# Attention in pairs: the routing table's fill one store a chunk, scatters only behind it, early weights later

## The chip, the cores and the metric

The kernel runs on one core of a Trainium2 chip. The metric is the device time of one launch in microseconds (us); the time of a kernel is the median of several runs. Engines: TensorE (PE, matrix products; PEld is its weight load), VectorE (DVE), ScalarE (ACT), GpSimd (POOL) and SyncE (SP, which issues most DMAs).

## The reference

Three layers follow each other, all in float32. Batch 8, 8 heads, 576 positions, head width 64; afterwards 4608 tokens of width 512.

```python
# 1 retention: scores with a decay by distance, no softmax
ret = scale * (q @ k.T) * Dmat          # Dmat[i,j] = gamma_h**(i-j) for i >= j, else 0
x = (ret @ v)                           # then tokens x 512
# 2 top-1 mixture of 8 experts
logits = x @ w_gate + modality_bias[modality_id]
e_idx = argmax(logits); gate_w = softmax(logits)[e_idx]
out[mask] = gate_w[mask] * (relu(x[mask] @ w1[e]) @ w2[e])      # for each expert e
# 3 soft mixture of 8 experts with 4 slots each
logits = out @ phi
slot_input = softmax(logits, over tokens).T @ out
slot_out[e] = relu(slot_input[e] @ w1_[e]) @ w2_[e]
y = softmax(logits, over slots) @ slot_out
```

## The kernel before, in words

**Stages.** The attention stage computes x and the routing, the second stage the experts over at most 43 slots of 128 tokens, the third the soft mixture. The change lies in the attention stage alone.

**Chunks and pairs.** Two batch entries make 9 chunks of 128 tokens (8 of one entry each, and a ninth, shorter one of both ends), so there are 36 chunks `g`. The loop at `P_` handles two of them at a time: pair a has the chunks a and b = a+1, and the pairs are named here by their even chunk (pair 2, pair 4, ... pair 32; a last pair, 34, is written out behind the loop). In each pair stand, in this order: `loads(a); loads(b)`; `emit_v` for b and a+2 (line 167: vh, the scaled values, on GpSimd); score products `emit_S(a)` (line 176) and their masks (line 179, VectorE); products with the running state (`emit_cross`, line 200); gate logits of pair a−4; `emit_tok` of the pair before (line 218: x turned on TensorE, copied to xr by ScalarE at line 219, stored to xd in DRAM at lines 220 and 222); `emit_S(b)`; the gate products; values (`emit_AV`, line 205) and state products (`emit_state`, line 188, with ScalarE's state copy at line 189) in turn: AV(a), state(b), AV(b), state(a+2); the scaling of x (line 210); and pieces of the routing chain (`tick`, lines 232 to 259, among them r_ob at line 239 and the indices idx at line 257). Then come the scatters, and in pairs 24 to 30 `split`, which cuts a weight in `raw` into a high and a low part.

**Routing table.** `tb` in DRAM holds one row of 16 floats for each place of 128*324. `fill_tb` (line 156) writes the filler value into a ninth of it, from a tile `none` that shares its memory with `w2T1`. `scatter(k)` (lines 261 and 262) writes the 128 tokens of chunk k into their places by an indirect DMA of GpSimd, behind a small memset of `spare`. Rows of two scatters never meet, so scatters don't wait for each other; each waits for the fill and for its indices. A scatter's instruction stands in GpSimd's queue, in order, with the vh products. Four chunks are routed together: those of chunks 4k to 4k+3 can be scattered from pair 4k+8 on.

**DMA order.** SyncE issues its DMAs in the order of the program: `loads(g)` gives chunk g+5's kqv (7 buffers), then the extras that the change moves; the xd stores of the pair before come behind both. xr has 2 buffers, so a pair's xr copy waits until the store of the pair before has been read out. ScalarE is in order too: the state copies of a pair stand behind its two xr copies. state products accumulate in one PSUM tile, so state(a+2) waits for the state copy of b.

**Early weights.** `load_W(e)` brings expert e's w2T in four pieces of 0.5 MiB: e=0 into `w2`, e=1 into `w2T1`, e=2 into `raw` behind the splits, e=3 into kqv buffers. They are read behind the last pair. Four pieces of expert 0's w1 go into `raw` for the splits.

Of the kernel before, what the change touches and what calls it, by code (L numbers as in the profile page):

```python
# [80 lines left out]
def body(nc,tc,I,O):  # L81
# [3 lines left out]
    def nodep(ins,key):  # L85
        i=ins.ins if hasattr(ins,'ins') else ins
        if key in nodeps: tc.declare_no_dep(i,group=key,reason="the rows of one scatter differ from every other's")
        tc.add_to_no_dep_group(key,i); nodeps[key]=1
    ctx=ExitStack()
    with ctx, tc.manual_schedule():  # L90
# [8 lines left out]
        raw=[WP.tile([128,2048],F32,name=f"raw{j}") for j in range(2)]; w2=WP.tile([128,8,512],F32,name="w2")  # L99
# [18 lines left out]
        def load(g,xs=None):  # L118
            if g not in kqv: kqv[g]=A1.tile([128,4,512],F32,name="kqv",bufs=NKQ)
            for x,y in xs or ((0,3 if g%NCH==8 else 4),): SP.dma_start(out=kqv[g][:,x:y],in_=I['qkv'][g,:,x:y])  # L120
# [13 lines left out]
        def rest():  # L134
            SP.dma_start(out=cm[:,128:],in_=I['cm'][:,128:516]); SP.dma_start(out=tri,in_=I['tri']);
            SP.dma_start(out=mid,in_=I['mid'].bitcast(I32).rearrange("p (t w) -> p t w",w=2))
            SP.dma_start(out=mb.rearrange("p m e -> p (m e)"),in_=I['mb'].to_broadcast([128,2*E]))
        def decay(c):
            for h in range(2 if c==4 else 1):
                s=slice(64*h,64*h+64) if c==4 else slice(0,128); w=s.stop-s.start  # L140
                G_.tensor_tensor(out=gt[:,c,:,s],in0=gt[:,0,:,0:w],in1=bc(gr[:,:,c],[128,NP,w],2),op=ALU.mult)
# [14 lines left out]
        def fill_tb(): SP.dma_start(out=tb.rearrange("(k p c) w -> k p c w",p=128,k=TC//36)[tbk.pop(0)],in_=none)  # L156
# [5 lines left out]
        def tick(n=1,stop=True):  # L162
            for _ in range(n):
                if rq and not (stop and rq[0].__name__=="rank"): rq.pop(0)()
        def emit_v(g):
            t=A1.tile([128,H,D],F32,name="vh",bufs=3)
            G_.tensor_tensor(out=t,in0=kqv[g][:,2].rearrange("p (h d) -> p h d",h=H),in1=bc(vtab[:,pos_(g)],[128,H,D],2),op=ALU.mult)  # L167
            vh[g]=t
# [54 lines left out]
        def emit_logit(g):  # L223
            c=8*(g-max(k for k,_ in GR if k<=g))
            PE.matmul(out=psm[:,c:c+8],lhsT=lss[g//2][:,128*(g%2):128*(g%2)+128],rhs=sel[:,0:E],start=True,stop=True)
        rt={}
        def route_a(k0,n):
            ks=slice(k0,k0+n); sh=[128,n,E]
            def T(name,shape=sh,dt=F32): return A2.tile(shape,dt,name=name)
            l,mx,dl,ex,oh,ix,ob=T("r_l"),T("r_mx",[128,n]),T("r_d"),T("r_e"),T("r_oh"),T("r_ix",[128,n]),T("r_ob",dt=BF16)  # L230
            rt[k0]=(ex,ix,ob)
            return [lambda: V.tensor_tensor(out=l,in0=psm[:,0:n*E].rearrange("p (n e) -> p n e",e=E),in1=bias[:,ks],op=ALU.add),
                lambda: V.tensor_reduce(out=mx,in_=l,axis=AX.X,op=ALU.max),
                lambda: V.tensor_tensor(out=dl,in0=l,in1=bc(mx,sh,2),op=ALU.subtract),
                lambda: A.activation(out=ex,in_=dl,func=AF.Exp),

                lambda: V.scalar_tensor_tensor(out=oh,in0=dl,scalar=0.0,in1=bc(e8,sh,1),op0=ALU.is_equal,op1=ALU.mult),
                lambda: V.tensor_reduce(out=ix,in_=oh,axis=AX.X,op=ALU.max),
                lambda: V.tensor_tensor(out=ob,in0=bc(e8,sh,1),in1=bc(ix,sh,2),op=ALU.is_equal)]
        def route_b(k0,n):  # L240
            ks=slice(k0,k0+n); sh=[128,n,E]; ex,ix,ob=rt.pop(k0)
            def T(name,shape=sh,dt=F32): return A2.tile(shape,dt,name=name)
            rk=psm[:,40:40+n*E].rearrange("p (n e) -> p n e",e=E); rs,po,sm=T("r_rs"),T("r_po",[128,n]),T("r_sm",[128,n])
            r=[a for a,_ in GR].index(k0)
            if k0<GR[-1][0]: cn=T("r_cn",[128,E])
            def rank():
                PE.matmul(out=rk,lhsT=tri[:,:128],rhs=ob,start=True,stop=False)
                PE.matmul(out=rk,lhsT=tri[:,128:],rhs=bc(cum[:,r],sh,1),start=False,stop=n==1)
                for c in range(n-1): PE.matmul(out=rk[:,c+1:],lhsT=tri[:,128:],rhs=bc(ob[:,c],[128,n-1-c,E],1),start=False,stop=c==n-2)
            return [lambda: V.tensor_reduce(out=sm,in_=ex,axis=AX.X,op=ALU.add),  # L250
                lambda: V.tensor_scalar(out=sm,in0=sm,scalar1=1e-9,scalar2=None,op0=ALU.add),
                lambda: V.reciprocal(out=gk[:,ks,1],in_=sm),
                rank,
                lambda: V.tensor_tensor(out=rs,in0=rk,in1=ob,op=ALU.mult),
                lambda: V.tensor_reduce(out=po,in_=rs,axis=AX.X,op=ALU.add),

                lambda: V.scalar_tensor_tensor(out=idx[:,ks],in0=ix,scalar=float(36*128),in1=po,op0=ALU.mult,op1=ALU.add)]+([] if k0==GR[-1][0] else [
                lambda: V.tensor_reduce(out=cn,in_=ob.rearrange("p n e -> p e n"),axis=AX.X,op=ALU.add),  # L258
                lambda: V.tensor_tensor(out=cum[:,r+1],in0=cum[:,r],in1=cn,op=ALU.add)])
        def scatter(k):  # L260
            G_.memset(spare,0.0)
            nodep(G_.indirect_dma_start(out=tb,out_offset=bass.IndirectOffsetOnAxis(ap=idx[:,k:k+1],axis=0),in_=gk[:,k],in_offset=None),"tb")  # L262
# [6 lines left out]
        def load_W(e,cs=range(4)):  # L269
            if e not in w2T: w2T[e]={}  # L270
            for c in cs:
                if e in(3,5):
                    if c%2==0: w=A1.tile([128,2,1024],F32,name=f"w2T{e}",tag="kqv",bufs=NKQ); w2T[e].update({c:w[:,0],c+1:w[:,1]})
                elif e==2: w2T[e][c]=raw[c//2][:,c%2*1024:c%2*1024+1024]
                else: w2T[e][c]=(w2T1 if e==1 else w2)[:,2*c:2*c+2].rearrange("p a f -> p (a f)")
                SP.dma_start(out=w2T[e][c],in_=I['w2T'][e,:,c])
# [14 lines left out]
        scat=[]  # L291
        def logit(g):
            emit_logit(g)
            def f(k0,n): rq.extend(route_a(k0,n)+[lambda: rq.extend(route_b(k0,n)+[lambda: scat.extend(range(k0,k0+n))])])
            for k0,n in GR[:-1]:
                if g==k0+n-1: f(k0,n)
        def loads(g):
            if g==0: load(4)
            if g+5<NT: load(g+5)
            if 4<=g<10: fill_tb(); fill_tb() if g%2 else 0  # L300
            if g==1: rest()
            if g==5: SP.dma_start(out=phi,in_=I['phi'])
            if 10<=g<26 and g%2==0: load_W((g-10)//8,[(g-10)//2%4])
            if g in(15,17,19,21): x,y=divmod(g//2-7,2); SP.dma_start(out=raw[x][:,1024*y:1024*y+1024],in_=I['w1'][0,:,x,1024*y:1024*y+1024])
            if g in(30,31,33): load_W(2,{30:[0],31:[1],33:[2,3]}[g])
            if g in(32,33): load_W(3,range(2*g-64,2*g-62))
        emit_v(0); emit_S(0); emit_state(0)
        for P_ in range(NT//2-1):
            a,b=2*P_,2*P_+1; ready=rq and rq[0].__name__=="rank"
            loads(a); loads(b)  # L310
            emit_v(b); emit_v(a+2)
            for g in (a,b):
                if g<4: decay(g+1)
            for _ in range(3 if a==4 else 2):
                if prepare and a: prepare.pop(0)()
            if a: emit_S(a)
            emit_cross(a); emit_cross(b)
            for g in (a-4,b-4):
                if g>=0: logit(g)
            if ready: tick(1,False)  # L320
            if a: emit_tok(a-2); emit_tok(b-2)
            tick(4)
            emit_S(b)
            if a: emit_gate(P_-1)
            emit_AV(a)
            if b%NCH<8: emit_state(b)
            emit_AV(b)
            if (a+2)%NCH<8: emit_state(a+2)
            emit_x(a); emit_x(b)
            tick(14)  # L330
            for _ in range(2):
                if scat: scatter(scat.pop(0))
            for g in (a,b):
                if 24<=g<32: split((g-24)//4,[(g-24)%4])

# [8 lines left out]
        a,b=NT-2,NT-1; ready=rq and rq[0].__name__=="rank"  # L344
# [258 lines left out]
        for i in range(NSURE):  # L603
            slot(i)
            x,h=divmod(i-12,2)
# [114 lines left out]
```

## Time and profile before

| what | us |
|---|---|
| median of 3 runs (650.27 to 654.31) | 653.67 |
| the profiled execution, whole | 657.15 |
| its span, first to last instruction | 655.1 |
| TensorE busy in the span | 598.1 |
| of the span: from the start of pair 4 to that of pair 34 | 24.53 to 156.26 |

The profile is of one execution. Times in its rows count from the start of the span. Busy time of an engine leaves out its queue's waits; "idle before" is the time in which an engine stood, and the name behind the arrow is what ended it by the profile: of several things waited for, the one that came last among those that the trace shows. A DMA's landing has no row of its own; a SyncE row is the issue alone.

### The profile page before, as it was taken

What the parts mean: (1) busy time and instruction counts of PE and PEld (TensorE: products, weight loads), DVE (VectorE), ACT (ScalarE), POOL (GpSimd) and SP (SyncE); (2) the same over time, 40 slices, a digit from 0 to 9 for tenths busy, and PEclk for the clock granted to TensorE, in tenths of its full rate; (3) what the DMA queues carried; (4) which work ended last, traced back from release to release, by engine and by line L of the source; (5) the groups of instructions that cost most, each with busy time, mean ns of one, the idle gap of its engine ahead of it and who ended that gap; (6) DMA issues with size and microseconds to landing.
All of it is one profiled execution on the core that took longest, in us unless ns stands there. A gap on an engine that the chain in (4) does not pass through costs nothing. (4 is left out here: it accounts for less than half of the span.)

```text
span 655.1 us, 17160 instructions
## 1 busy us (share of the span) xinstructions
PE 598.1 (91%) x6005; PEld 445.0 (68%) x6005; DVE 317.2 (48%) x952; ACT 202.6 (31%) x528; POOL 239.3 (37%) x347
## 2 busy tenths in 40 slices
PE   7996999999796999998899999999999999769984
PEld 5775888887465667775577777777776777543553
DVE  1554666666523343566354555544556445422343
ACT  1212222332124233264223332332345223212232
POOL 3614555543444323366233433444346333210000
PEclk7999999999899899998899999999999999989995
DMA  8999999999358570036634444434335401399888
GB/s 306 405 409 403 362 395 416 410 347 336 101 181 313 193 307 17 21 99 217 245 133 160 163 166 165 148 129 152 140 101 165 154 20 28 108 354 388 334 288 289
DMA packets 48243, 148.47 MB, mean 227 GB/s; under 512 B 12276, under 2 KB 24063, under 8 KB 37888
## 3 DMA queue, kind: packets, MB, share of 16 engines
q1 hardware_dynamic: 41936, 132.54, 55.1%
q0 software_dynamic: 6192, 14.53, 6.2%
q8 instruction: 57, 0.93, 0.6%
q14 instruction: 58, 0.48, 0.2%
HBM read 276.14 MB, written 27.71 MB: 464 GB/s over the span
## 5 line engine op out<-in xcount | busy, mean ns | idle before, releaser
L489 PE MATMUL ps_L<-wh,xl 128*128 128x512 f32 x624 | 211.4, 409 | 0.1
L489 PEld LDWEIGHTS ps_L<-wh,xl 128*128 128x128 f32 x624 | 115.9, 191 | 36.8 <-issue 16.3
L489 PE MATMUL ps_L<-wl,xl 128*128 128x512 f32 x312 | 127.0, 407 | 12.2 <-POOLq L546 6.3
L489 PEld LDWEIGHTS ps_L<-wl,xl 128*128 128x128 f32 x312 | 59.3, 190 | 41.2 <-POOL cy L525 16.1
L493 DVE TENSOR_SCALAR hh<-ps_L,gi 128x512 f32<-128x512 f32 x39 | 29.3, 750 | 101.0 <-PE ps_L L489 101.0
L511 ACT ACTIVATE z<-ps_z,mt 32x128 f32<-32x128 f32 x39 | 14.0, 358 | 156.5 <-DVE mt L510 156.5
L179 DVE TENSOR_TENSOR st_s<-ps_s,cm 128x512 f32<-128x512 f32 x72 | 46.2, 683 | 31.2 <-PE ps_s L176 18.3
L525 POOL TENSOR_SCALAR cy<-cx,cm 128x32 f32<-128x32 f32 x39 | 15.0, 384 | 121.1 <-DVE cm L524 117.2
L262 POOL DMA_INDIRECT tb<-gk,idx x36 | 35.6, 988 | 53.8 <-DVE r_cn L258 30.6
L167 POOL TENSOR_TENSOR vh<-kqv,vtab 128x512 f32<-128x512 f32 x36 | 37.2, 1040 | 40.3 <-PE ps_x L205 25.3
L526 POOL DMA_INDIRECT cs<-cy,ui x39 | 43.0, 1103 | 16.9 <-POOL cy L525 13.3
L176 PE MATMUL ps_s<-kqv 64*128 64x128 f32 x576 | 45.8, 294 | 0.0
L498 PE MATMUL ps_h<-cs__100,hh 128*128 128x128 f32 x312 | 41.3, 275 | 1.2 <-DVE hh L493 1.2
L219 ACT COPY xr<-ps_t 128x512 f32<-128x512 f32 x36 | 20.2, 587 | 71.0 <-DMA xd<-xr 23.2
L176 PEld LDWEIGHTS ps_s<-kqv 64*128 64x128 f32 x576 | 38.0, 195 | 6.0 <-issue 2.7
L205 PE MATMUL ps_x<-st_s,vh 128*64 128x128 f32 x576 | 40.0, 281 | 0.0
L210 DVE TENSOR_TENSOR xT<-ps_x,gt 128x512 f32<-128x512 f32 x36 | 23.2, 686 | 33.7 <-PE ps_x L205 32.0
L205 PEld LDWEIGHTS ps_x<-st_s,vh 128*64 128x64 f32 x576 | 32.0, 139 | 7.5 <-issue 7.2
L498 PEld LDWEIGHTS ps_h<-cs__100,hh 128*128 128x128 f32 x312 | 35.6, 142 | 1.8 <-DVE hh L493 1.6
L470 POOL DMA_INDIRECT xr__2796<-xd,ui x28 | 29.3, 1047 | 16.4 <-POOL ui L469 7.8
L492 ACT ACTIVATE hh<-ps_L,gi 128x512 f32<-128x512 f32 x39 | 26.9, 689 | 25.9 <-PE ps_L L489 25.7
L469 POOL CAST ui<-gi 128x1 uint32<-128x1 f32 x42 | 7.6, 182 | 67.8 <-DMA cs<-cy,ui 56.9
(234 smaller groups left out, 967.6 us busy)
## 6 DMA issues: line engine op xcount, KB each, us to landing
raw<-in_w SPq DMA_DIRECT2D x79, 1024.0 KB
w<-in_w SPq DMA_DIRECT2D x38, 2048.0 KB
kqv<-in_qkv SPq DMA_DIRECT2D x28, 1024.0 KB
m<-in_m SPq DMA_DIRECT2D x19, 1024.0 KB
xd<-xr SPq DMA_DIRECT2D x32, 256.0 KB
w2T<-in_w2T SPq DMA_DIRECT2D x12, 512.0 KB
out<-m SPq DMA_DIRECT2D x12, 512.0 KB
mx<-in_m SPq DMA_DIRECT2D x5, 1024.0 KB
```

The source lines that it names most:

```text
L167: G_.tensor_tensor(out=t,in0=kqv[g][:,2].rearrange("p (h d) -> p h d",h=H),in1=bc(vtab[:,pos_(g)],[128,H,D],2),op=ALU.mult)
L176: r=slice(64*h,64*h+64); PE.matmul(out=pss[h][:,p],lhsT=pk(g,0)[r,p],rhs=pk(g,1)[r,p],start=True,stop=True)
L179: V.tensor_tensor(out=st,in0=pss[h],in1=bc(masks[g%NCH],[128,NP,128],1),op=ALU.mult)
L205: PE.matmul(out=xo(g,p,h),lhsT=v[:,2*p+h],rhs=sts[g,h][:,p],start=False,stop=p>1,skip_group_check=True)
L210: V.tensor_tensor(out=of(xTs[g//2],g).rearrange("q (h n) t -> q h n t",h=2),in0=xps[g//2][:,:,256*(g%2):256*(g%2)+256].rearrange("q h (n t ...
L262: nodep(G_.indirect_dma_start(out=tb,out_offset=bass.IndirectOffsetOnAxis(ap=idx[:,k:k+1],axis=0),in_=gk[:,k],in_offset=None),"tb")
L470: G_.indirect_dma_start(out=xg[i%3],out_offset=None,in_=xd,in_offset=bass.IndirectOffsetOnAxis(ap=u,axis=0),bounds_check=NTOK-1,oob_is_err ...
L489: PE.matmul(out=ps,lhsT=a[:,c],rhs=w[h][:,s],start=n==0,stop=n==11); n+=1; m+=1
L492: if h==0: A.activation(out=d,in_=q,func=AF.Relu,scale=g)
L493: else: V.tensor_scalar(out=d,in0=q,scalar1=0.0,scalar2=g,op0=ALU.max,op1=ALU.mult)
L498: for c in range(4): PE.transpose(out=ps[:,c],in_=hh[i%2][:,2*half+c//2,(c%2)*128:(c%2)*128+128],identity=ident)
L526: nodep(G_.indirect_dma_start(out=cs,out_offset=bass.IndirectOffsetOnAxis(ap=gi[i][1],axis=0),in_=y,in_offset=None,bounds_check=NTOK-1,oob ...
```

## The change

Three things, all in the pair loop. The nine fill stores, issued at chunks 4 to 9 (one at even, two at odd chunks), are issued at chunks 5 to 13, one each. The scatters, up to two a pair from pair 8 on, are up to three a pair from pair 14 on. Weight pieces move: experts 0 and 1 of w2T from the even chunks 10 to 24 to chunks 20, 21, 23, 24, 26, 27, 29 and 30; the four pieces of w1 from chunks 15, 17, 19, 21 to 14, 15, 17, 18; expert 2 of w2T from chunks 30, 31, 33 (1, 1 and 2 pieces) to 32 and 33 (2 each).

```diff
+        W1_=[14,15,17,18]; W01=[20,21,23,24,26,27,29,30]
         def loads(g):
             if g==0: load(4)
             if g+5<NT: load(g+5)
-            if 4<=g<10: fill_tb(); fill_tb() if g%2 else 0
+            if 5<=g<14: fill_tb()
             if g==1: rest()
             if g==5: SP.dma_start(out=phi,in_=I['phi'])
-            if 10<=g<26 and g%2==0: load_W((g-10)//8,[(g-10)//2%4])
-            if g in(15,17,19,21): x,y=divmod(g//2-7,2); SP.dma_start(out=raw[x][:,1024*y:1024*y+1024],in_=I['w1'][0,:,x,1024*y:1024*y+1024])
-            if g in(30,31,33): load_W(2,{30:[0],31:[1],33:[2,3]}[g])
+            if g in W01: k=W01.index(g); load_W(k//4,[k%4])
+            if g in W1_: x,y=divmod(W1_.index(g),2); SP.dma_start(out=raw[x][:,1024*y:1024*y+1024],in_=I['w1'][0,:,x,1024*y:1024*y+1024])
+            if g in(32,33): load_W(2,range(2*g-64,2*g-62))
             if g in(32,33): load_W(3,range(2*g-64,2*g-62))
...
             tick(14)
-            for _ in range(2):
-                if scat: scatter(scat.pop(0))
+            if a>13:
+                for _ in range(3):
+                    if scat: scatter(scat.pop(0))
```

On GpSimd, from pair 6 on, the queue before had the first scatters right behind pair 8's vh products (`DMA tb` is a scatter, 41472 the rows of the table):

```order
L167 TENSOR_TENSOR vh<-kqv,vtab 128x512 x4
L261 MEMSET spare 1x1
L262 DMA tb<-gk,idx 41472x16
L261 MEMSET spare 1x1
L262 DMA tb<-gk,idx 41472x16
L167 TENSOR_TENSOR vh<-kqv,vtab 128x512 x2
L261 MEMSET spare 1x1
L262 DMA tb<-gk,idx 41472x16
```

Now, at the same place:

```order
L167 TENSOR_TENSOR vh<-kqv,vtab 128x512 x10
L261 MEMSET spare 1x1
L262 DMA tb<-gk,idx 41472x16
L261 MEMSET spare 1x1
L262 DMA tb<-gk,idx 41472x16
L261 MEMSET spare 1x1
L262 DMA tb<-gk,idx 41472x16
L167 TENSOR_TENSOR vh<-kqv,vtab 128x512 x2
```

The vh products of pairs 10 to 14 now stand ahead of the first scatter, and three scatters stand between the vh products of pairs 14 and 16.

On SyncE, from pair 4's loads to pair 8's first one, the queue before was (`tb<-w2T_98` is a fill store):

```order
L120 DMA kqv<-in_qkv 128x2048
L156 DMA tb<-w2T_98 128x576
L120 DMA kqv<-in_qkv 128x2048
L156 DMA tb<-w2T_98 128x576 x2
L302 DMA phi<-in_phi 128x128
L220 DMA xd<-xr 128x512 x2
L120 DMA kqv<-in_qkv 128x2048
L156 DMA tb<-w2T_98 128x576
L120 DMA kqv<-in_qkv 128x2048
L156 DMA tb<-w2T_98 128x576 x2
L220 DMA xd<-xr 128x512 x2
L120 DMA kqv<-in_qkv 128x2048
```

Now:

```order
L120 DMA kqv<-in_qkv 128x2048 x2
L156 DMA tb<-w2T_98 128x576
L303 DMA phi<-in_phi 128x128
L220 DMA xd<-xr 128x512 x2
L120 DMA kqv<-in_qkv 128x2048
L156 DMA tb<-w2T_98 128x576
L120 DMA kqv<-in_qkv 128x2048
L156 DMA tb<-w2T_98 128x576
L220 DMA xd<-xr 128x512 x2
L120 DMA kqv<-in_qkv 128x2048
```

Ahead of the xd stores of pair 6 stand three fill stores instead of six.

## Rows read from the trace of the kernel before

**Rows 1.** The page's first line.
```profile
span 655.1 us, 17160 instructions
```

**Rows 2.** Stretches cut at pair starts: us, busy by engine, clock, DMA share, GB/s.
```profile
24.53:34.29 9.76, 7.89 (x136) 6.62 (x132) 4.88 (x8) 2.09 (x5) 6.76 (x11) 1.00 1.01 408
34.29:41.91 7.62, 7.62 (x135) 6.45 (x132) 3.34 (x8) 1.92 (x6) 1.04 (x1) 1.00 1.04 414
41.91:51.75 9.84, 8.09 (x155) 6.88 (x153) 6.41 (x18) 2.01 (x6) 1.07 (x2) 1.00 1.02 400
51.75:64.32 12.57, 8.95 (x151) 7.60 (x148) 4.08 (x10) 2.31 (x6) 5.54 (x9) 0.94 1.01 404
64.32:73.91 9.59, 9.59 (x140) 8.02 (x138) 6.88 (x15) 2.19 (x5) 6.20 (x9) 0.90 0.99 365
73.91:89.76 15.85, 15.85 (x304) 13.84 (x301) 9.61 (x27) 4.14 (x10) 7.90 (x12) 1.00 1.00 367
89.76:129.97 40.21, 39.61 (x707) 34.06 (x703) 25.53 (x66) 11.81 (x29) 21.32 (x32) 1.00 1.02 415
```

**Rows 3.** TensorE in order of time: start, us, instruction, idle before and releaser.
```profile
51.14 0.69 PE L188 MATMUL ps_st<-vh,kqv 128*64 128x64 f32 x16 [1.36 <-issue]
...
61.72 0.69 PE L188 MATMUL ps_st<-vh,kqv 128*64 128x64 f32 x16 [3.62 <-POOL vh L167]
...
64.32 2.08 PE L176 MATMUL ps_s<-kqv 64*128 64x128 f32 x16
...
73.91 1.16 PE L176 MATMUL ps_s<-kqv 64*128 64x128 f32 x16
```

**Rows 4.** GpSimd in order of time.
```profile
58.14 1.18 POOL L262 DMA_INDIRECT tb<-gk,idx  x1 [14.94 <-DVE st_s L179]
...
60.62 2.04 POOL L167 TENSOR_TENSOR vh<-kqv,vtab 128x512 f32<-128x512 f32 x2
...
65.17 2.04 POOL L167 TENSOR_TENSOR vh<-kqv,vtab 128x512 f32<-128x512 f32 x2
...
81.69 1.04 POOL L167 TENSOR_TENSOR vh<-kqv,vtab 128x512 f32<-128x512 f32 x1 [0.30 <-PE ps_x L205]
...
85.87 1.01 POOL L262 DMA_INDIRECT tb<-gk,idx  x1 [3.12 <-DVE r_cn L258]
...
88.91 2.04 POOL L167 TENSOR_TENSOR vh<-kqv,vtab 128x512 f32<-128x512 f32 x2 [0.75 <-PE ps_x L205]
```

**Rows 5.** ScalarE in order of time.
```profile
49.25 1.23 ACT L219 COPY xr<-ps_t 128x512 f32<-128x512 f32 x2 [7.06 <-DMA xd<-xr]
...
50.65 0.39 ACT L189 COPY st<-ps_st 128x256 f32<-128x256 f32 x1
...
77.94 1.07 ACT L219 COPY xr<-ps_t 128x512 f32<-128x512 f32 x2 [3.55 <-PE ps_t L218]
```

**Rows 6.** SyncE in order of time: issues of DMAs.
```profile
40.94 1.00 SPq L220 DMA_DIRECT2D xd<-xr  x2
...
47.03 1.35 SPq L156 DMA_DIRECT2D tb<-w2T  x2
```

**Rows 7.** VectorE in order of time.
```profile
45.68 0.16 DVE L257 SCALAR_TENSOR_TENSOR idx<-r_ix,r_po 128x4 uint32<-128x4 f32 x1
...
64.99 2.27 DVE L239 TENSOR_TENSOR r_ob<-cm,r_ix 128x32 bf16<-128x32 f32 x1
...
83.06 0.19 DVE L239 TENSOR_TENSOR r_ob<-cm,r_ix 128x32 bf16<-128x32 f32 x1
```

**Rows 8.** The page's DMA issues: how many, KB each.
```profile
kqv<-in_qkv SPq DMA_DIRECT2D x28, 1024.0 KB
...
xd<-xr SPq DMA_DIRECT2D x32, 256.0 KB
...
tb<-w2T SPq DMA_DIRECT2D x9, 288.0 KB
...
raw<-in_w SPq DMA_DIRECT2D x4, 512.0 KB
```

## The prediction

> **What bounds the kernel now.** I read the page first: the profiled execution spans 655.1 us and took 657.15 us; three timed runs have a median of 653.67 us [rows 1]. The change touches only the attention stage, so the next view is the table of stretches, cut at the starts of the pairs (a pair starts with the first score matmul of its even chunk) [rows 2]. A pair that nothing holds takes TensorE 7.62 us (the stretch from 34.29). Pair 8 takes 9.84, pair 10 takes 12.57 and pair 12 takes 9.59: 2.22, 4.95 and 1.97 too long. In all of them the DMA share is about 1.0 at 400 to 414 GB/s, so the queue is full as well; that matters below.
>
> Two chains make those losses. The order in time on TensorE shows the first state matmuls of pair 8's end starting at 51.14 after 1.36 us of idle, and those of pair 10 at 61.72 after 3.62 us waiting for vh [rows 3].
> - **Scatter behind the fill.** On GpSimd the first scatter starts at 58.14 after 14.94 us of idle; behind it in the same queue stand the vh products that pair 10 needs, which run at 60.62 [rows 4]. The row names VectorE as releaser, but the scatter's indices were written at 45.68 [rows 7]. What else it needs is the table it writes into: the last two fill stores were issued at 47.03 [rows 6]. So the wait is for the fill to land, some 10 us after issue.
> - **Row store ahead of the state copy.** ScalarE's copy xr at 49.25 waited 7.06 us for an xd store, and the state copy stands behind it at 50.65 [rows 5]; TensorE needs that one at 51.14. The xd store in question was issued at 40.94 [rows 6]: 8.3 us from issue until the buffer was free, which at the 400 to 408 GB/s of that stretch is about 3.3 MB ahead of it in the queue.
>
> Pair 12's loss is a consequence: after the 3.62 us of idle the granted clock of pairs 10 and 12 is 0.94 and 0.90 in the mean [rows 2], and 16 score matmuls take 2.08 us where they take 1.16 in pair 14 [rows 3], close to the ratio of the 1.2 and 2.4 GHz levels. VectorE's r_ob also took 2.27 us instead of 0.19 while two vh products ran [rows 4, 7].
>
> **The change part by part.**
>
> *The scatters leave pairs 8 to 12.* Six scatters of about 1.2 us each (two of them fill the time from 85.87 to 88.16, 0.75 us ahead of the vh at 88.91 [rows 4]) go to later pairs, and with them the wait of 14.94 us. vh of pair 10 then runs right behind that of pair 8. Of pair 10's 4.95 us I keep 0.3 for what is late next, the xr copy (below): 4.65 us saved. Without the idle the clock doesn't fall and r_ob meets no late vh: of pair 12's 1.97 us I keep 0.3 too: 1.67 us.
>
> *The fill spread thin.* A pair issues two kqv loads of 1 MiB and two xd stores of 0.25 MiB [rows 8]; the fills of 0.28 MiB come on top: three in each of pairs 4, 6 and 8 before, one, two, two, two, two in pairs 4 to 12 now. At pair 6's xd store 0.84 MiB (0.88 MB) less has been issued: at 408 GB/s it lands 2.2 us earlier, so pair 8's xr runs at 47.1 instead of 49.25. TensorE without its 1.36 us of idle would have been ready at 49.78, and copy to state takes 51.14 − 49.25 = 1.9 us, so xr is in time until 47.9, 6.0 us after the pair's start. The wait goes; I keep 0.2 of the pair's 2.22: 2.0 us. Pair 4's long 9.76 us stays: its xr waits for stores that stand ahead of the first fill in both kernels.
>
> Sum of the early part: 2.0 + 4.65 + 1.67 = 8.3 us.
>
> *The weights later.* The queue is what may take this back. A pair of 7.62 us at 408 GB/s moves 2.97 MiB; 2.5 are kqv and xd, so 0.47 MiB of extras fit. Extras in MiB, pairs 4 to 32: before 0.84, 0.84, 0.84, 0.5, 0.5, then 1, 1, 1, 1, 0.5, 0.5, 0, 0, 1, 3; now 0.28, 0.56, 0.56, 0.56, 0.56, then 1, 0.5, 0.5, 1, 0.5, 0.5, 1, 0.5, 0.5, 4. In pairs 14 to 24 the new kernel brings 4.0 MiB for a room of 2.8 + 0.25 (one short kqv chunk): 0.95 MiB over, 2.4 us. Before it was 5.0 MiB, 1.95 over, 5.0 us; but its queue had run partly dry during the stalls: 365 and 367 GB/s over 25.4 us [rows 2] are about 1.05 MB less than 408 would be, 2.6 us. So both come to the same 2.4 us. What differs is where they start: before, xr of pair 14 ran at 77.94, 4.0 us after the pair's start and unhurried [rows 5]; now it will stand about 5.5 us after it, near the limit. That 1.5 us of slack is used up, so later pairs pay up to 1.5 us more: between −1.5 (all of it paid) and 0 (the five pairs from 89.76 at 8.04 us a pair had waits of their own [rows 2], which then may shrink). I take −1.4, nearest to the ledger.
>
> The four weight pieces put into raw at chunks 14 to 18 come before the splits of pair 24 need them. Pieces 20 to 30 are read only behind the last pair. All 4 MiB at pair 32 (3 before) stand ahead of its xd stores, 2.6 us more; no state copy follows in the last pair, so 0 to −1, taken as 0.
>
> *Three scatters a pair from pair 14.* Three cost 3.6 us, two vh 2.04 [rows 4]: 5.6 of 7.62 us on GpSimd, so vh is not held up by number. What is queued behind the first scatter is pair 16's vh, and TensorE waits for that. The last fill is now issued in pair 12, which starts at about 41.9 + 7.8 + 7.9 = 57.6; with the old latency of 58.14 − 47.03 = 11 us it lands near 68.5, while GpSimd gets there soon after pair 14's start, at 66. Three scatters then end near 72, some 1 us after vh could have begun, and vh is not needed until about 5 us later. The one thing in its way is r_ob of pair 16: 83.06 in the old trace, when GpSimd was past its vh [rows 7]. Bounds 0 and 2.27 − 0.19 = 2.1 us; I take 0.3, since only part would overlap. A 27th scatter inside the loop takes one from the end, where they wait for the last indices anyway: 0.
>
> Result: 8.3 − 1.4 − 0.3 = 6.6 us. For the profiled execution 657.15 − 6.6 = 650.5; for the median 653.67 − 6.6 = **647.1 us**. Nothing behind the attention stage changes, so the gain should arrive whole.
>
> **Rivals.**
> - *Nothing is given back.* The waits of the later pairs (8.04 against 7.62 us [rows 2]) shrink as much as the lost slack costs: 8.3 us, at most 10 with some of those waits gone: 645.4. For it: 2 MiB less has been issued by pair 18. Against it: the DMA share stays at 1.0 there. Chance 0.16.
> - *The queue gives back more.* If 365 to 367 GB/s from 64 to 90 us is not a dry queue but what it gives with scatters and weights together, the new kernel meets that rate too and loses the 2.6 us of the ledger: gain 4.0, 649.7. Against it: 415 GB/s in the next five pairs, with scatters and weights [rows 2]. Chance 0.22. The Trainium skill's rule on this speaks against the change as a whole: in "DMA: Bandwidth & Descriptors", section Bandwidth, the share of one core binds loads from HBM near 358 GB/s. By that share a pair would move 2.6 MiB, the room for extras would be 0.1, and every pair of either kernel would stand at the queue. The 366 GB/s of these two stretches come near it; the 400 to 415 of the others disagree, and the same page gives 425 to a core that streams alone.
> - *GpSimd's late vh blocks VectorE.* In pair 12 r_ob stood for 2.27 us beside two vh products. In pair 16 the second vh ends at 81.69 + 1.04 = 82.73 and r_ob starts at 83.06: 0.3 us between [rows 4, 7]. If the third scatter puts vh later than that in the five pairs that route (16, 20, 24, 28, 32), each pays what pair 12 paid, 1.97 us: −9.9, so 6.6 − 9.9 = −3.3: 657.0, slower. It decides from vh starting over 0.3 us later than now; the 5.6 us of work in 7.62 speak against it. Chance 0.05. The skill states such a lock in "SBUF — State Buffer", section Who interferes with whom: VectorE with two SBUF inputs and a GpSimd operation that reads SBUF exclude each other; the row on r_ob agrees.
> - *The change doesn't do what it says.* If the first scatter waited for something other than the fill, the wait returns at pair 14 with its 4.65 and 1.67 us: gain 8.3 − 6.3 = 2.0 less the queue's 1.4: 653.1. Against it: no other operand was late. Chance 0.06.
>
> **How the numbers follow.** The forecast case, gain 5 to 8 us (645.7 to 648.7), has 0.51. About 1% (6.5 us) is what a measurement of this kernel tells from no change. Over that lie the first rival (0.16) and somewhat over half of the forecast (0.29): faster 0.45. Within lie the rest of the forecast (0.22), the second rival (0.22) and the last (0.06): same 0.50. Slower 0.05. The range runs from 643.5 (nothing given back and 1.7 of the later waits gone) to 651.5 (the second rival with 1 us at the end and 0.8 of collision).
>
> **What would show it.** Right: no idle of GpSimd ahead of a scatter before pair 14 and under 4 us there; TensorE's waits for vh from pair 10 on gone; pairs 8, 10, 12 between 7.6 and 8.0 us with clock 1.00; xr in pairs 12 to 24 still waiting for xd. Wrong: pairs 14 to 30 longer than before by over 3 us in sum, a DMA rate under 395 GB/s there, r_ob near 2 us in several pairs, or a new wait of TensorE at pair 16.

## The result and the profile after

Timed beside the kernel before, the changed kernel took 647.98 us in the median of 10 runs (646.22 to 648.78), the kernel before 653.99 us (10 runs, 650.27 to 656.13): a ratio of 0.9908, with a 95% interval of 0.9886 to 0.9931. The forecast was 647.1 us. Two later sets of runs, each on one chip with its own runs of the kernel before, did not repeat it: 660.02 against 657.25 us (1.0037, 1.0016 to 1.0058) and 658.91 against 657.48 us (1.0022, 1.0002 to 1.0042). So there are two things to explain: why the forecast came out, and why the gain went away elsewhere.

The profiled execution of the first measurement took 648.3 us; its page begins:

```profile
span 646.5 us, 17164 instructions
```

The stretches that answer to [rows 2], cut at the starts of pairs 4, 6, 8, 10, 12, 14, 18 and 28, with the same columns:

```profile
25.80:35.59 9.79, 7.90 (x137) 6.62 (x133) 4.88 (x8) 2.10 (x5) 6.76 (x11) 1.00 1.01 410
35.59:43.20 7.61, 7.61 (x135) 6.45 (x132) 3.34 (x8) 2.31 (x6) 1.04 (x1) 1.00 1.04 376
43.20:51.47 8.27, 7.88 (x156) 6.88 (x154) 5.39 (x16) 1.82 (x4) 2.33 (x3) 1.00 1.02 410
51.47:59.55 8.08, 8.08 (x152) 7.02 (x148) 4.70 (x12) 2.31 (x6) 2.08 (x3) 1.00 1.03 414
59.55:67.33 7.78, 7.78 (x142) 6.72 (x138) 5.05 (x16) 2.19 (x5) 2.09 (x3) 1.00 1.02 388
67.33:84.49 17.16, 16.87 (x306) 14.14 (x302) 10.66 (x27) 4.12 (x10) 10.45 (x17) 1.00 1.02 404
84.49:125.36 40.87, 39.75 (x707) 33.97 (x703) 25.49 (x66) 11.77 (x29) 25.20 (x39) 1.00 1.02 396
```

Pairs 8, 10 and 12 fell from 9.84, 12.57 and 9.59 us to 8.27, 8.08 and 7.78, with the clock at 1.00; pairs 14 and 16 grew from 15.85 to 17.16, and the five behind them from 40.21 to 40.87.

On TensorE, in order of time (as [rows 3]), the state products at the ends of pairs 8 and 10 no longer stand idle first:

```profile
50.91 0.64 PE L188 MATMUL ps_st<-vh,kqv 128*64 128x64 f32 x16
...
58.99 0.63 PE L188 MATMUL ps_st<-vh,kqv 128*64 128x64 f32 x16
```

GpSimd in order of time (as [rows 4]), the first scatters and the vh behind them:

```profile
71.98 1.18 POOL L262 DMA_INDIRECT tb<-gk,idx  x1 [3.84 <-DMA kqv<-in_qkv]
...
73.46 0.97 POOL L262 DMA_INDIRECT tb<-gk,idx  x1 [0.20 <-issue]
...
74.74 0.96 POOL L262 DMA_INDIRECT tb<-gk,idx  x1 [0.22 <-issue]
75.72 2.06 POOL L167 TENSOR_TENSOR vh<-kqv,vtab 128x512 f32<-128x512 f32 x2
```

SyncE's last fill store (as [rows 6]), and r_ob of pair 16 on VectorE (as [rows 7]):

```profile
62.55 0.34 SPq L156 DMA_DIRECT2D tb<-w2T  x1
```

```profile
76.77 1.06 DVE L239 TENSOR_TENSOR r_ob<-cm,r_ix 128x32 bf16<-128x32 f32 x1
```

The first scatter waits 3.84 us, until 9.4 us behind the last fill's issue, and vh follows the three scatters while r_ob runs beside it. ScalarE (as [rows 5]), two of its row copies:

```profile
48.33 1.23 ACT L219 COPY xr<-ps_t 128x512 f32<-128x512 f32 x2 [5.51 <-DMA xd<-xr]
...
82.03 1.21 ACT L219 COPY xr<-ps_t 128x512 f32<-128x512 f32 x2 [5.84 <-DMA xd<-xr]
```

Pair 8's copy runs 5.1 us after the pair's start instead of 7.3. Later copies now wait for their stores where pair 14's did not before. In pair 18 this reaches TensorE. ScalarE and then TensorE, which stands 0.34 us and begins the state product 0.1 us after the state copy has ended:

```profile
90.11 1.21 ACT L219 COPY xr<-ps_t 128x512 f32<-128x512 f32 x2 [5.08 <-DMA xd<-xr]
...
91.60 0.38 ACT L189 COPY st<-ps_st 128x256 f32<-128x256 f32 x1
```

```profile
92.08 0.69 PE L188 MATMUL ps_st<-vh,kqv 128*64 128x64 f32 x16 [0.34 <-issue]
```

In pair 30 the vh products are late. GpSimd's third scatter of pair 28 ends at 133.87 (its row is below), both vh follow at once, and cum, a step of VectorE's routing chain that takes 0.21 us in this pair of the kernel before, takes 1.05 us beside them; TensorE then waits for VectorE's masks. GpSimd, VectorE, TensorE:

```profile
133.90 2.04 POOL L167 TENSOR_TENSOR vh<-kqv,vtab 128x512 f32<-128x512 f32 x2
```

```profile
134.92 1.05 DVE L259 TENSOR_TENSOR cum<-cum,r_cn 128x8 bf16<-128x8 bf16 x1
```

```profile
137.84 1.75 PE L176 MATMUL ps_s<-kqv 64*128 64x128 f32 x16 [0.54 <-DVE st_s L179]
```

### The profile page after: what moved, and what is told of

It reads as the page before. It is cut to its first block, busy times and chain, and to the rows that moved or that the text cites. A ratio compares the mean times of both kernels' runs of the same rounds, so it can differ in the third digit from the quotient of the medians.

```text
span 646.5 us, 17164 instructions
## 1 busy us (share of the span) xinstructions
PE 595.1 (92%) x6005; PEld 443.9 (69%) x6005; DVE 316.6 (49%) x952; ACT 202.7 (31%) x528; POOL 239.5 (37%) x347
```

## The experiments

Three sets of four kernels, each set on a chip of its own, together with its runs of the kernel before. The table gives the profiled executions by pairs: us from one pair's first score matmul to that of the pair behind the last one named. The ratios are to the kernel before in the same set. A profile is of one execution, and not of the median one: e1's took 654.42 us, the shortest of its 12 runs, e2's 663.42, its longest.

| kernel | pairs 4, 6 | pairs 8 to 12 | pairs 14 to 32 | median us | ratio (95%) |
|---|---|---|---|---|---|
| before, first profile | 17.38 | 32.00 | 82.35 | 653.99 | |
| changed, first profile | 17.40 | 24.13 | 84.29 | 647.98 | 0.9908 (0.9886 to 0.9931) |
| set 1: before | | | | 656.87 | |
| e1 scatters alone | 17.35 | 26.33 | 91.35 | 657.85 | 1.0022 (1.0000 to 1.0044) |
| e2 fill and scatters | 22.78 | 24.20 | 92.06 | 657.48 | 1.0002 (0.9974 to 1.0031) |
| e3 weights alone | 19.42 | 30.24 | 81.93 | 657.05 | 0.9995 (0.9972 to 1.0019) |
| e4 changed, 4 row buffers | 15.28 | 24.12 | 88.94 | 650.85 | 0.9921 (0.9888 to 0.9953) |
| set 2: before | | | | 657.25 | |
| e5 changed | 20.50 | 24.16 | 91.33 | 660.02 | 1.0037 (1.0016 to 1.0058) |
| e6 changed, 2 scatters a pair | 18.08 | 24.12 | 87.56 | 664.25 | 1.0099 (1.0068 to 1.0131) |
| e7 as e1, 2 scatters a pair | 20.11 | 25.58 | 86.08 | 666.60 | 1.0117 (1.0079 to 1.0155) |
| e8 changed, scatters from pair 16 | 21.84 | 24.12 | 91.28 | 657.73 | 1.0007 (0.9975 to 1.0039) |
| set 3: before | | | | 657.48 | |
| e9 before | 17.18 | 32.45 | 83.26 | 657.35 | 0.9988 (0.9969 to 1.0007) |
| e10 changed | 23.53 | 24.20 | 93.34 | 658.91 | 1.0022 (1.0002 to 1.0042) |
| e11 changed, no scatter in the loop | 20.88 | 24.12 | 81.74 | 686.72 | 1.0455 (1.0431 to 1.0480) |
| e12 changed, scatters apart | 23.71 | 24.28 | 87.61 | 653.22 | 0.9933 (0.9911 to 0.9956) |

### Set 1: the parts of the change alone

e1 is the kernel before with the scatters moved; e2 adds the fill; e3 has the weights' edit alone; e4 is the changed kernel with two more buffers for the row copies, taken from memory that is idle in this stage.

```diff
# e1
-            for _ in range(2):
-                if scat: scatter(scat.pop(0))
+            if a>13:
+                for _ in range(3):
+                    if scat: scatter(scat.pop(0))
# e2: the same, and
-            if 4<=g<10: fill_tb(); fill_tb() if g%2 else 0
+            if 5<=g<14: fill_tb()
# e4: the changed kernel, and
-            xr=A1.tile([128,DM],F32,name="xr",bufs=2); A.copy(out=xr,in_=xp)
+            xr=A1.tile([128,DM],F32,name="xr",bufs=2) if g%4<2 else Wall[:,2*(g%4):2*(g%4)+2].rearrange("p e s -> p (e s)"); A.copy(out=xr,in_=xp)
```

Expected of e1: 

> The kernel before with only the scatters moved (up to three a pair from pair 14 on); fill stores and weights as before. Theory (two chains and a full DMA queue): GpSimd's 14.9 us wait goes, pair 10 falls from 12.57 to 8.0 to 8.5 us and pair 12 from 9.59 to 7.8 to 8.2; pair 8 stays near 9.8, because its xr still waits behind six fill stores; the queue, no longer emptied by the stall, takes 2 to 4 us back in pairs 14 to 26. About 650.5 to 652. Rival one (nothing is taken back by the queue): 647.5. Rival two (the fill stores' density is the cause and the scatter only a bystander): no change, pair 10 stays over 11 us.

Expected of e2: 

> The changed kernel with the weights' pieces at the chunks of before (10 to 24 and so on): fill and scatters alone. Theory (bytes ahead in the queue set the later pairs): 1 MiB more is issued by pair 12 and 2 MiB more by pair 18 than in the changed kernel, so xr comes later and pairs 10 to 24 take 2 to 4 us more in sum: 650 to 652. Rival (moving the weights is worth nothing, as they are hidden anyway): 648, pairs 10 to 24 within 0.5 us of the changed kernel's.

Expected of e3: 

> The kernel before with only the weights' pieces moved. Theory: pair 10 keeps its wait for vh behind the scatter (12 us), pair 8 its wait for xr (9.8 us), as nothing ahead of pair 8's stores has changed; the waits of pairs 20 to 24 (8.25, 8.09) shrink to about 7.7, up to 1.5 us gained: 652 to 653.5. Rival (the weights are the main part of the gain): below 650.

Expected of e4: 

> The changed kernel with four xr buffers in place of two (two of them in memory of Wall that is unused until the end of the stage), so that a pair's xr copies need the store of two pairs earlier, not one. Theory (what is left of the loss comes through the xr copy that waits for the xd store): ScalarE's waits for xd go, pair 4 falls from 9.8 to about 7.7 us, pairs 8, 10, 14 to 22 and 30 to 7.6 to 8.0; 4 to 6.5 us gained on the changed kernel: 641.5 to 644. Rival one (the queue itself binds, loads of kqv come late instead): TensorE waits for kqv or vh, 646 to 648. Rival two (the later pairs are long by VectorE's and GpSimd's order, not by xd): only pair 4 gains, 646.

Measured: moving the scatters does repair pairs 10 and 12 (8.47 and 7.77 us in e1), and pair 8 stays at 10.09 us there, where the changed kernel, with equally short pairs 4 and 6 and the fill spread, has 8.27. In e2 pair 8 is 8.26 too, but its pairs 4 and 6 had lost 5.4 us already, so that e2 doesn't separate the fill: in e3 and e7, with the old fill, pair 8 is 8.26 as well, where pairs 4 and 6 had taken 19.42 and 20.11. The weights alone leave pairs 10 and 12 as they were (12.87 and 9.11) and don't change the time. But no part alone made the kernel faster: what e1 and e2 gain in pairs 8 to 12 they lose again in pairs 14 to 32, 9.0 and 9.7 us against the first profile of before. e4 takes away ScalarE's waits for row stores and keeps a gain; its pairs 4 and 6 are the shortest of all, but pairs 14 to 32 take 88.94 us, 4.7 more than in the changed kernel's first profile, where the copies waited. Where the loss stands was not among the expected things: for the most part in pairs 16, 20, 28 and 32, with gaps of TensorE inside groups of matmuls, mostly with the releaser "issue", that is, waiting for nothing that the profile shows. That became the question.

### Set 2: how many scatters, and the changed kernel again

```diff
# e6: the changed kernel (e5), and     e7: e1, and
-                for _ in range(3):
+                for _ in range(2):
# e8: the changed kernel, and
-            if a>13:
+            if a>15:
```

Expected of e5: 

> The changed kernel as it is, beside the others on one chip. What is open: with the scatters moved alone (the first experiment) and with four row buffers (the fourth), TensorE stood in pairs 16, 20, 28 and 32 in gaps of 0.2 to 0.5 us, some 0.7 us apart, that the profile puts to no other engine, and these pairs took 9.5 to 11.8 us; the profile of the changed kernel has 8.2 to 8.8 us there. Theory T: the gaps come where three scatters stand back to back in a pair that routes and the row copies do not hold TensorE back; then the changed kernel has none of them here either: pairs 14 to 32 sum to 84 to 86 us and the ratio to before is 0.989 to 0.993. Rival C: the gaps belong to the chip that the first four experiments ran on, or come and go from one execution to the next: the changed kernel shows them as well if it lands there, pairs 14 to 32 at 88 us or more, ratio 0.995 or above.

Expected of e6: 

> The changed kernel with two scatters a pair from pair 14 on instead of three; 8 of the 28 scatters of the loop then stand behind it, at some 1.3 us each. Theory T (three back to back make the gaps): no unexplained gap of TensorE in pairs 16 to 32, those pairs as in the changed kernel or shorter, pairs 14 to 32 sum to 82.5 to 84.5 us; the stretch from pair 34 to the experts' first matmul is longer by up to 8 times 1.3 = 10 us, by 5 to 10 us in all, so the time is 652 to 657. Rival Q (bytes in the queue, not the number of scatters, set these pairs): the sum stays within 0.5 us of the changed kernel's, and only the end moves.

Expected of e7: 

> The kernel before with scatters from pair 14 on alone, two a pair instead of the three of the first experiment; fill and weights as before. Theory T: pairs 16, 20, 28 and 32 lose their gaps against the first experiment (11.76, 9.64, 10.51 and 10.47 us there) and come to 8 to 9.2 us; pairs 14 to 32 sum to 81.5 to 85 us where the first experiment had 91.4; pairs 10 and 12 stay at 8.5 and 7.8. Rival Q (the old places of the weights in the queue make the gaps): the four pairs stay at 9.5 us or more and the sum at 88 or more. The end is longer by 5 to 10 us in both cases.

Expected of e8: 

> The changed kernel with its first scatters one pair later (from pair 16 on, three a pair). If the wait of GpSimd for the fill costs anything in the changed kernel (3.84 us of idle ahead of the scatter at 71.98, then r_ob at 1.06 instead of 0.19 us in pair 16), that is gone: no idle ahead of the first scatter, r_ob 0.19, pair 16 shorter by 0.5 to 0.9 us; one scatter more at the end, 0 to 1.3 us. In all 1 us less to 0.8 more than the changed kernel on the same chip. Rival (that wait sits in GpSimd's slack and pair 16 is set by the row copies): pair 16 within 0.3 us of the changed kernel's, the time the same or up to 1.3 us longer.

Measured: the changed kernel itself has the gaps here, 91.3 us in pairs 14 to 32, and with them it is no faster than the kernel before. Fewer scatters a pair shorten these pairs (e6 87.6, e7 86.1, against 91.3 and 91.4 with three), but not as far as theory T said: pair 16 stays at 11.19 us in both, so two in a row can make gaps as well. The scatters left over for the end, 1.27 us apart there, cost more than that: the stretch from pair 34 to the experts' first matmul is 45.58 us in e6 and 35.36 in e5, 10.2 us for 7 scatters, so that e6 misses its expected 652 to 657 us by 7. In e8 r_ob of pair 16 is back at 0.19 us, and pair 16 takes 8.71 us where e5 has 11.94, but the gaps come later instead (pair 18 at 10.86, pair 32 at 10.64). Its first scatter still waited 4.88 us, up to 82.19, though its last fill was issued at 62.74: that wait is not the fill's; the profile names VectorE's masks (st_s) as its releaser, and what it is stays open.

### Set 3: no scatters, and scatters apart

```diff
# e11: the changed kernel (e10), and
-            if a>13:
+            if a>99:
# e12: the changed kernel, and
-            emit_v(b); emit_v(a+2)
+            emit_v(b)
+            if a>15 and scat: scatter(scat.pop(0))
+            emit_v(a+2)
+            for _ in range(2):
+                if a>15 and scat: scatter(scat.pop(0))
...
-            if a>13:
+            if a==32:
```

Expected of e9: 

> The kernel before as it is, for its pairs on the same chip as the next three, since the changed kernel gained 6.0 us where it was first timed and lost 2.8 in the fifth experiment. Theory S: TensorE's gaps in the routing pairs (0.2 to 0.5 us, about 0.7 us apart, waiting for nothing that the profile shows) come two to three us behind the start of a run of scatters that follow each other on GpSimd; two scatters a pair make few of them. Then pairs 14 to 32 sum to 82 to 84.5 us here and pairs 8 to 12 to 30 to 33, as in its first profile. Rival C (a slower chip, whatever the scatters): its pairs 14 to 32 are at 87 us or more as well.

Expected of e10: 

> The changed kernel once more, beside the kernel before on a chip that need not be the one of the fifth experiment. Pairs 8 to 12 at 24 to 25 us in every case. If the row copies wait for their stores in pairs 14 to 26 as in its first profile: few gaps, pairs 14 to 32 at 84 to 86 us, ratio 0.989 to 0.993. If they don't wait, as in the fifth experiment: gaps in pairs 16, 20, 28 and 32, the sum at 88 to 94 us, ratio 0.998 to 1.006.

Expected of e11: 

> The changed kernel with no scatter in the loop: all 36 stand behind it. Theory S: no gap of TensorE without a releaser in pairs 14 to 32, the sum of these pairs 80.5 to 83 us whatever the changed kernel itself has on this chip; the end longer by 27 times 1.27 = 34 us or some less, and in pair 34 gaps only if scatters run beside it. Rival Q (the queue or the chip make the gaps): the sum within 1 us of the changed kernel's on this chip, with its gaps in the same pairs.

Expected of e12: 

> The changed kernel with its three scatters a pair taken apart on GpSimd: one between the two vh products of the next pair and two behind them, so that they don't wait for indices in the middle of a pair and no three follow each other directly. If it is the unbroken row of three that makes the gaps: pairs 16, 20, 28 and 32 within 0.5 us of the kernel before, pairs 14 to 32 at 81 to 84.5 us, and the time 5 to 9 us below the kernel before. If the number of scatters in a pair makes them, wherever they stand: the sum within 1.5 us of the changed kernel's on this chip, and the time within 2 us of it.

Measured, by the stretches from the start of pair 14 to that of pair 34 (columns as in [rows 2]), first e9, then e10, e11 and e12:

```profile
74.64:157.90 83.26, 82.14 (x1444) 69.74 (x1441) 53.96 (x139) 25.82 (x61) 41.54 (x62) 1.00 0.98 375
```

```profile
71.04:164.38 93.34, 88.45 (x1445) 73.51 (x1441) 54.38 (x140) 26.11 (x61) 49.08 (x76) 0.96 0.95 360
```

```profile
69.79:151.53 81.74, 81.22 (x1446) 69.68 (x1442) 53.63 (x139) 25.79 (x61) 20.97 (x22) 1.00 1.00 394
```

```profile
72.24:159.85 87.61, 83.08 (x1444) 70.14 (x1441) 59.70 (x140) 26.06 (x61) 49.98 (x76) 1.00 1.00 387
```

The third and fourth differ from the second in the place of the scatters alone. Without them TensorE needs 81.74 us for the same pairs on the same chip, 11.6 less, in a DMA queue that is as full (share 1.00). So the gaps come with the scatters, as theory S has it, and neither the queue nor the chip makes them alone.

The gaps are not all of the loss. Pair 16 of e10 takes 13.31 us against 8.16 in e11; its gaps sum to about 1.2 us, and behind them the granted clock falls: it is 0.74 in the mean of the pair, and 16 score matmuls take 2.08 us there instead of 1.16. Nor does every row of three make gaps: in pairs 18 and 22 of e10 three scatters follow each other as closely, from 1.06 and 0.92 us behind the pair's start, and these pairs take 7.93 and 7.99 us without one. What the other pairs add was not found.

What one looks like: pair 28 of e10, TensorE and then GpSimd in order of time:

```profile
142.13 0.46 PE L205 MATMUL ps_x<-st_s,vh 128*64 128x128 f32 x4
142.90 0.49 PE L205 MATMUL ps_x<-st_s,vh 128*64 128x128 f32 x5 [0.30 <-issue]
144.35 0.67 PE L205 MATMUL ps_x<-st_s,vh 128*64 128x128 f32 x7 [0.97 <-issue]
```

```profile
139.83 1.01 POOL L262 DMA_INDIRECT tb<-gk,idx  x1 [4.20 <-DVE r_cn L258]
...
141.14 0.97 POOL L262 DMA_INDIRECT tb<-gk,idx  x1 [0.21 <-issue]
...
142.42 0.97 POOL L262 DMA_INDIRECT tb<-gk,idx  x1 [0.23 <-issue]
```

The 16 value products belong to one chunk and wait for nothing of each other; they run as 4, 5 and 7, from 142.13 to 145.02 instead of in 1.05 us. The gaps begin beside the third scatter, 2.8 us behind the start of the first. The same pair of the changed kernel's first profile, with the scatters at the same distance, has none:

```profile
132.62 1.05 PE L205 MATMUL ps_x<-st_s,vh 128*64 128x128 f32 x16
```

```profile
130.32 1.01 POOL L262 DMA_INDIRECT tb<-gk,idx  x1 [4.19 <-DVE r_cn L258]
...
131.63 0.97 POOL L262 DMA_INDIRECT tb<-gk,idx  x1 [0.21 <-issue]
...
132.90 0.97 POOL L262 DMA_INDIRECT tb<-gk,idx  x1 [0.22 <-issue]
```

Such pairs are the larger part of the difference between a gain and none (the rest is in pairs 4 and 6), and why that first timing was spared is not settled (below).

In e12 no three scatters follow each other in pairs 16 to 30. Pair 20 of it, GpSimd and TensorE:

```profile
97.60 1.05 POOL L167 TENSOR_TENSOR vh<-kqv,vtab 128x512 f32<-128x512 f32 x1
...
98.85 1.01 POOL L262 DMA_INDIRECT tb<-gk,idx  x1 [0.18 <-issue]
...
100.16 0.97 POOL L262 DMA_INDIRECT tb<-gk,idx  x1 [0.21 <-issue]
103.84 1.04 POOL L167 TENSOR_TENSOR vh<-kqv,vtab 128x512 f32<-128x512 f32 x1 [2.71 <-PE ps_x L205]
```

```profile
99.68 1.07 PE L218 MATMUL ps_t<-cs__100,xT 128*128 128x128 f32 x8
100.69 1.16 PE L176 MATMUL ps_s<-kqv 64*128 64x128 f32 x16
102.08 0.64 PE L214 MATMUL ps_m<-xT,wg 128*32 128x256 f32 x8 [0.23 <-DVE r_rs L254]
```

Pair 20 takes 8.52 us (9.63 in e10), and of pairs 14 to 32 only pair 32 has unexplained gaps: there, at the end of the loop, three scatters do stand in a row, and it takes 11.04 us. e12 is 5.7 us below e10 on the same chip and is the only version that was faster than the kernel before in sets 2 and 3, by 4.3 us where 5 to 9 were expected. It misses its expected 84.5 us by 3.1, of which pair 32 is the largest piece (11.04 against 9.18 in e9); the rest are waits of TensorE for VectorE, which is busy for 59.70 us in these pairs, against 53.63 in e11. e12 also moves the scatters within the pair, to 1.9 and 3.2 us behind the start of pair 20 where e10 has them from 0.9 us on; e6 has two in a row from 0.9 us and small gaps there (pair 20 at 8.81 us), so the runs don't separate the unbroken row from the place. Four row buffers and scatters apart in one kernel were not tried.

## Why the prediction came out, point by point

- **Scatters leave pairs 8 to 12.** Right in mechanism and size. Forecast 2.0, 4.65 and 1.67 us, measured 1.57, 4.49 and 1.81; the sum is 7.9 us in the first profile and 8.2 in set 3 (32.45 against 24.20), and e1 shows that for pairs 10 and 12 it is the scatters. The clock term is right too: without the idle it stays at 1.00. Pair 8's copy came 5.1 us after the pair's start, as forecast (47.1 less 41.91). The yardstick of 7.62 us was too short for pair 8: it takes 8.26 to 8.27 us in every profile in which it doesn't wait for the copy, so it stayed above the 7.6 to 8.0 us that I had named as a sign of being right.
- **The weights' and the queue's payback.** In the first profile pairs 14 to 32 grew by 1.94 us, where I had 1.4 for this and 0.3 for the scatters. The mechanism is there at half the size: late copies hold TensorE in pair 18, as shown above, and in pair 22 in the same way (0.39 us), and these two pairs are 0.7 us longer than before. Elsewhere the copies were late and TensorE needed nothing of them. So the step that was sized wrong is "that 1.5 us of slack is used up, so later pairs pay up to 1.5 us more". In e11, with the same weights and the same full queue, row copies wait for stores in most of the pairs from 16 to 30 (4.85 us in pair 16), and these pairs take no more than in the kernel before on that chip (81.74 against 83.26 us); e3 has the weights alone and 81.93 us.
- **Three scatters a pair.** This is the term that was mis-sized and, for its larger part, of another mechanism. I asked whether the scatters would hold up vh, and gave the collision of r_ob 0.3. In pair 16 r_ob did take 1.06 us instead of 0.19, within the bounds, and cost nothing: the matmuls that need it began 2.62 us behind the pair's start in both kernels. In pair 30 vh was late, VectorE's cum met the same collision, and the pair is 0.8 us longer than before. The Trainium skill, "SBUF — State Buffer", section Who interferes with whom, has a VectorE instruction with two SBUF inputs and a GpSimd instruction that reads SBUF exclude each other; both rows agree. But the scatters also slow and stop TensorE itself, which no term had. In the first profile that is at most the 1.3 us by which pairs 14 and 16 grew (of pair 16's 1.01 us, e11 has 0.39 without scatters); pairs 28 and 32 became 0.8 us shorter, for which I have no reason. Against the 81.74 us without scatters, pairs 14 to 32 took 2.55 us more in the first profile, 9.6 in e5 and 11.6 in e10.
- **The end, at 0.** From pair 34 to the experts' first matmul: 34.83 us before and 32.36 after, 33.95 in e9 and 32.71 in e10, but 35.36 in e5. It was 1.2 to 2.5 us shorter in the first two comparisons and not in e5, so the runs show no steady change here.
- **Rivals.** "The change doesn't do what it says" did not happen, nor did the r_ob rival in the five pairs that it named; cum in pair 30 is the one case of its mechanism. "Nothing is given back" was the queue's case: in e11 the queue gave nothing back, and in e10, on the same chip, the time went elsewhere. The case that ended on the other side in sets 2 and 3, scatters that stop TensorE, was not among the rivals. No gap in the pairs of the first trace hinted at it: the 0.22 us in pair 22, also put to "issue", stand ahead of a state product behind a late copy, like those of pair 18 above.

So the sum was right where it was first timed, but only in part for its reasons. The pairs from 4 to 32 gave 5.9 us in the profiles, against 6.6 forecast, with one loss half as large as forecast and others in its place. That these came out near the forecast sum is luck, and so is part of how near the time came: the two profiled executions differ by 8.85 us (657.15 and 648.30) and the medians by 6.0. In the changed kernel's profile pair 4 began 1.3 us later, and all that stands behind pair 32 took 4.0 us less. From the experts' first matmul on, where nothing was changed, the fourteen profiles take 459.8 to 464.0 us. In sets 2 and 3 the same early gain is there and the loss behind it is larger: by the sign that I had named for being wrong, pairs 14 to 30 longer by over 3 us, the forecast is wrong in e5 and e10 (by 7.5 and 8.7 us longer).

**The early pairs.** The second reason is in pairs 4 and 6, which ended before any scatter. e9 and then e10, stretches of pairs 4 and 6:

```profile
25.01:34.57 9.56, 7.89 (x137) 6.62 (x133) 4.88 (x8) 2.10 (x5) 6.77 (x11) 1.00 1.02 412
34.57:42.19 7.62, 7.62 (x136) 6.46 (x133) 3.34 (x8) 1.86 (x6) 1.04 (x1) 1.00 1.01 402
```

```profile
23.31:35.47 12.16, 8.32 (x136) 7.00 (x132) 4.88 (x8) 2.10 (x5) 8.03 (x15) 0.91 1.02 403
35.47:46.84 11.37, 11.37 (x134) 9.78 (x132) 3.34 (x8) 2.42 (x6) 1.04 (x1) 0.64 1.03 396
```

In e10 TensorE began pair 4 1.7 us earlier and so stood 3.84 us for the row copy's store instead of 1.67; then the granted clock was 0.64 through pair 6. The stores that this copy waits for were issued ahead of the first fill in both kernels, so I put this down to the start of an execution and not to the change; that was not tested by itself. For it: e3 and e7 have the old fill, and 9.18 and 9.22 us in pair 6, at a granted clock of 0.81 in both.

**What stays open.** Why the first timing of the changed kernel had hardly any gaps, in 10 runs within 2.6 us, is not shown. Two things go together in the profiles: there, ScalarE's row copies waited 3.9 to 5.8 us for their stores in five of the seven pairs 14 to 26, and in e4, e5 and e10, which have the gaps, none of them did. But in e1 pair 16 has such a wait and gaps as well, and so has pair 16 of e7, where the copies of six pairs in a row wait (14 to 24). In pair 32 the copy runs 3.4 us behind the pair's start in the first profile and in e10, and only e10 has gaps. The first timing may have been on another chip, and the kernel before was faster there too (653.99 against 656.87 to 657.48 us); no run sets one against the other.

## What to carry to other kernels

- An instruction that costs its own engine 1 us can cost another engine more. Price a moved or gathered group of indirect DMAs by what the other engines do beside it, not by the issuing engine's time alone, and try it with other work in between.
- A gain of 1% that hangs on one execution's order of events needs a second chip. Here the first 10 runs agreed within 0.4%, and the next 24, on two chips, showed no gain.
- A term of a forecast that comes out in size is not confirmed by that: e11 had the late copies behind the 1.4 us without their cost, and in the first profile they made 0.7 us of it.
- A gap put to "issue" is not always unexplained. Look at what stands just before it on the engine that makes its operand: ahead of a state product it was ScalarE's state copy.

## What the runs showed of the hardware

**A long row of scatters nearly stops TensorE.** e11 has 28 scatters in a row, 1.27 us apart, beside pair 34. Its stretches just before and inside the row (columns as in [rows 2]):

```profile
149.00:151.00 2.00, 2.00 (x50) 2.00 (x47) 0.32 (x1) 0.58 (x2) 1.06 (x2) 1.00 1.03 414
...
162.00:187.00 25.00, 6.96 (x20) 4.64 (x18) 0.00 (x0) 0.00 (x0) 20.55 (x40) 0.50 0.04 7
```

20 matmuls in 25 us, where there had been 50 in 2 us, at a DMA share of 0.04: the queue is empty, so it is not bandwidth. TensorE in order of time, inside the row and at its end, and GpSimd's last scatter of it:

```profile
168.35 0.37 PE L176 MATMUL ps_s<-kqv 64*128 64x128 f32 x1 [1.04 <-issue]
169.07 0.37 PE L176 MATMUL ps_s<-kqv 64*128 64x128 f32 x1 [0.36 <-issue]
171.18 0.37 PE L176 MATMUL ps_s<-kqv 64*128 64x128 f32 x1 [1.74 <-issue]
...
188.76 0.37 PE L176 MATMUL ps_s<-kqv 64*128 64x128 f32 x1 [2.43 <-issue]
189.47 0.57 PE L176 MATMUL ps_s<-kqv 64*128 64x128 f32 x1 [0.34 <-issue]
```

```profile
185.73 0.97 POOL L262 DMA_INDIRECT tb<-gk,idx  x1 [0.22 <-issue]
```

The matmuls of one group, which wait for nothing of each other, come one at a time, here 0.72 and 2.11 us apart, and the group ends only behind the last scatter. The first gap begins 2.4 us behind the start of the first scatter. The DMA queues from 162 to 189 us (packets, MB, share of the engines' time):

```profile
q0 software_dynamic: 658, 0.17, 3.6%
q1 hardware_dynamic: 6, 0.02, 0.2%
```

No packet of an instruction queue starts in this time, though the whole profile of every run here has two such queues; the last one before it ends at 162.85, and the next begins at 203.30. The Trainium skill, "Runtime: NRT & Kernel Launch", section Instruction fetch mechanics, has each engine's sequencer fetch its instructions by a DMA queue of its own, in blocks, ahead of use. TensorE went on without a block arriving, so a late block was not what it waited for. The same holds in pair 20 of e10: its gaps lie from 103.8 to 106.2 us, and no instruction packet from 99 to 109. Which part of a scatter holds TensorE back (its descriptors, its packets or its signals) was not tried.
